# FNet mixing and a SoLU layer on one core: u transposed by block turns and block transfers instead of on TensorE

## The chip, the cores and the metric

The kernel runs on one core of a Trainium2 chip. The metric is the device time of one execution in microseconds (us); the median of three executions is 1578.13 (1572.94 to 1578.56). The engines are named as in the profile: PE is TensorE (PEld its weight loads), DVE is VectorE, ACT is ScalarE, POOL is GpSimd, and SP issues transfers. SP's transfers are also called its DMA queue (SPq).

## The reference

The input x has 8 sequences of 3136 rows with 256 features. The first block is the real part of a Fourier transform over rows and features. Its result, 25088 tokens of 256 features, goes through a layer of width 1024:

```
X = np.fft.fft(x, axis=1);  X = np.fft.fft(X, axis=2);  t = X.real
h = t @ w_in                                # 256 -> 1024
sm = softmax(h);  solu = h * sm
ln = (solu - mean) / sqrt(var + 1e-06) * g_ln
out = ln @ w_out                            # 1024 -> 256
```

## The kernel before, in words

All arithmetic is float32. The transform over 3136 = 49 x 64 rows is done in two steps. `transform1` (lines 134 to 157) works on a pair of sequences: 16 slices, each two matmuls against the table F; its result goes to DRAM (zd) and comes back turned (`turn`, lines 159 to 164: four transfers into g). `transform2` (166 to 176) is a matmul for each k1 of 25, and gives q, the stationary operand of the next matmul. The feature transform is folded into the weights Wi before the main loop. As x is real, the outputs for k1 and 49 - k1 come from the same q: an even and an odd part of h are computed, and their sum and difference are the two "signs" of a unit. So a unit is one pair of sequences and one k1, that is 128 tokens for each of two signs (for k1 = 0 one sign). There are 4 pairs x 25 units = 100 units.

For each unit: `up` (193 to 199) makes the two parts of h in PSUM (128 x 1024 each, one buffer each); `even` (201) copies the even part to SBUF; `join` (207) adds and subtracts on VectorE and takes the row maximum; `expo` (219) is the exponential on ScalarE, written to u; `product` (226) is u = h * u on VectorE, with its row sum; `square` (236) is ScalarE's sum of squares; `stats` (243) makes the row factor rs on GpSimd. The down product needs u with its 1024 features on the partitions. `transpose` (257 to 271) does that on TensorE: eight matmuls of 128 x 128 against an identity into PSUM, then two copies to SBUF (one ScalarE, one VectorE), giving uT. `down` (273) multiplies uT by Wo: eight matmuls with uT as the stationary operand and 256 moving columns; each float32 matmul stands as two in the profile. `store` (279) scales by rs and writes out: sign 0 by two plain transfers on SP's queue, sign 1 by an indirect transfer (scatter) on GpSimd's queue.

The order is written out by hand: instructions run on each engine in the order in which the loop of lines 421 to 460 issues them. A step of that loop does `up`, `join`, `expo`, `product` and `square` of the current unit, and `transpose`, `down` and `store` of the unit before it. Beside them it spreads the next pair's work (lines 383 to 402): `load` (94) brings a chunk of CH = 8 row positions twice, xa by a plain transfer and the mirrored xb by an indirect one; `add_mirror` (116) adds them on GpSimd; `fold` (124) folds the features on VectorE. Before the loop, the same is done for the first pair while the weights are prepared on VectorE (355 to 378).

## Time and profile before

| what | value |
|---|---|
| median of three runs | 1578.13 us (1572.94 to 1578.56) |
| time of the profiled execution | 1575.18 us |
| its span, first to last instruction | 1573.4 us |
| mean granted clock of TensorE | 0.969 |
| first and last start of `even` (L204) | 138.9 us, 1540.0 us |
| idle time of PE before L276 that ends with DVE's ot (L282) | 42.7 us |
| DMA packets, bytes | 45911, 84.72 MB |

A line of a group gives the line of the kernel, the engine, the operation, output <- inputs, the tile sizes and the count; behind the bar stand busy time in all, the mean of one in ns, and the idle time just before with what ended it. A line of the timeline gives start, duration, engine, line and operation, and in brackets the idle time before it with its releaser. Rows of the chain of waits give start, duration and what the chain went through. Rows of a window give its bounds and length, then busy time and count for PE, PEld, DVE, ACT and POOL, the granted clock, the mean busy share of the 16 DMA engines, and GB/s. Rows of a DMA queue give packets, MB and the share of the 16 engines' time. Matmuls overlap, so their rate is read from start to start.

### The profile page before, as it was taken

Reading aid. Unit: us, or ns where it says so; the run is one execution under the profiler, and the core shown is the slowest. Engines: PE = TensorE matmul, PEld = TensorE weight load, DVE = VectorE, ACT = ScalarE, POOL = GpSimd, SP = SyncE. Lnnn points to the kernel's source line nnn. Section 1 sums busy time; section 2 is a strip of 40 time slices with the busy share of each in tenths; the row PEclk is TensorE's granted clock in tenths of the full one; section 3 lists DMA queues with packets and bytes.
Section 4 is the critical chain, followed back from the end, with each engine's and each line's share of the span. In section 5 each row is a group of like instructions: output and inputs, shape, how many; then the busy total and the mean of one; then the engine's idle time right before and its main releaser. Section 6 shows DMA issues by size and latency. Waiting matters only on the chain.

```text
span 1573.4 us, 17844 instructions
## 1 busy us (share of the span) xinstructions
PE 1372.6 (87%) x6432; PEld 1043.2 (66%) x6432; DVE 965.8 (61%) x1725; ACT 621.2 (39%) x1049; POOL 413.0 (26%) x846
## 2 busy tenths in 40 slices
PE   2335999999999899999999899999999999999996
PEld 1213677777777677777777677777777677777775
DVE  3695656566655666565655756665655666666663
ACT  1101344344443443444443434434444434444442
POOL 3200323323213314223222324133212222221221
PEclk9667999999999999999999999999999999999998
DMA  9641212101052302101043402011023000000000
GB/s 230 201 85 41 59 38 64 39 21 38 18 111 75 96 20 82 38 21 38 21 89 65 129 18 85 22 34 38 21 70 72 18 21 21 20 17 21 19 19 20
DMA packets 45911, 84.72 MB, mean 54 GB/s; under 512 B 10390, under 2 KB 36638, under 8 KB 40832
## 3 DMA queue, kind: packets, MB, share of 16 engines
q1 hardware_dynamic: 33200, 52.64, 13.4%
q0 software_dynamic: 6656, 25.44, 5.2%
q10 hardware_dynamic: 5968, 5.52, 1.6%
q8 instruction: 50, 0.82, 0.2%
q14 instruction: 37, 0.30, 0.1%
HBM read 44.77 MB, written 38.80 MB: 53 GB/s over the span
## 4 chain that ended last, share of the span: by engine, by line
PE 56%; DVE 24%; issue 9%; ACT 8%; DMA 2%; DVEq 1%; POOL 1%; POOLq 0%; SPq 0%; ACTq 0%
PE ps_o L276 24%; PE ps_h L198 22%; DVE h L212 14%; ACT u L223 7%; PE tp L264 6%; PE ps L152 4%; DVE ot L282 2%; DVE ex L303 1%; DVE neg L217 1%; DMA xa<-in_x_dram 1%; DMA xb<-in_x_dram,idx 1%; DVE u L231 1%; POOL xa L121 1%; DVE rest L331 0%; DVE rest L333 0%
## 5 line engine op out<-in xcount | busy, mean ns | idle before, releaser
L276 PE MATMUL ps_o<-Wo,uT 128*128 128x256 f32 x3136 | 721.1, 383 | 44.7 <-DVE ot L282 42.7
L276 PEld LDWEIGHTS ps_o<-Wo,uT 128*128 128x128 f32 x3136 | 591.3, 191 | 181.5 <-issue 61.4
L223 ACT ACTIVATE u<-h,neg 128x1024 f32<-128x1024 f32 x196 | 223.6, 1142 | 434.3 <-DVE neg L217 434.3
L198 PE MATMUL ps_h<-Wi,q 128*128 128x512 f32 x800 | 379.2, 597 | 14.7 <-DVE q L180 14.7
L231 DVE SCALAR_TENSOR_TENSOR u<-h,u 128x1024 f32<-128x1024 f32 x196 | 239.2, 1220 | 130.9 <-ACT u L223 130.9
L233 POOL TENSOR_SCALAR nmean<-usum 128x1 f32<-128x1 f32 x196 | 55.8, 285 | 938.2 <-DVE u L231 938.1
L212 DVE CUSTOM_DVE_ANT_0 h<-ev,ps_h 128x1024 f32<-128x1024 f32 x196 | 231.7, 1219 | 81.6 <-PE ps_h L198 81.6
L240 ACT ACTIVATE h<-u,nmean 128x1024 f32<-128x1024 f32 x196 | 225.1, 1148 | 101.6 <-POOL nmean L233 99.0
L264 PEld LDWEIGHTS tp<-ident,u 128*128 128x128 f32 x1568 | 184.6, 142 | 62.3 <-issue 52.6
L270 ACT COPY uT<-tp 128x512 f32<-128x512 f32 x196 | 112.7, 575 | 280.8 <-PE tp L264 280.8
L282 DVE TENSOR_SCALAR ot<-ps_o,rs 128x256 f32<-128x256 f32 x196 | 94.4, 482 | 209.5 <-PE ps_o L276 209.5
L198 PEld LDWEIGHTS ps_h<-Wi,q 128*128 128x128 f32 x800 | 144.6, 191 | 117.5 <-issue 100.7
L264 PE MATMUL tp<-ident,u 128*128 128x128 f32 x1568 | 204.1, 273 | 0.0
L204 DVE SCALAR_TENSOR_TENSOR ev<-w_mid,q,ps_h 128x1024 f32<-128x1024 f32 x100 | 128.1, 1281 | 119.8 <-PE ps_h L198 119.8
L152 PE MATMUL ps<-y,F 98*100 98x258 f32 (+3 forms) x288 | 75.1, 398 | 81.5 <-DVE y L114 42.6
L268 DVE COPY uT<-tp 128x512 f32<-128x512 f32 x196 | 133.8, 683 | 1.2 <-PE tp L264 1.2
L285 POOL DMA_INDIRECT out_dram<-ot,idx x96 | 102.9, 1072 | 71.1 <-DVE ot L282 41.8
L152 PEld LDWEIGHTS ps<-y,F 98*100 98x100 f32 x288 | 44.0, 176 | 96.9 <-DVE ot L282 43.0
L121 POOL TENSOR_TENSOR xa<-xa,xb 98x2040 f32<-98x2040 f32 (+1 forms) x16 | 70.0, 4374 | 27.3 <-DMA xa<-in_x_dram 15.3
L255 POOL TENSOR_TENSOR rs<-v,neg_half 128x2 f32<-128x2 f32 (+1 forms) x100 | 71.8, 718 | 7.8
L172 PE MATMUL ps<-T,g 128*128 128x128 f32 x400 | 61.0, 275 | 0.0
L172 PEld LDWEIGHTS ps<-T,g 128*128 128x128 f32 x400 | 53.0, 191 | 0.7 <-issue 0.5
(57 smaller groups left out, 537.5 us busy)
## 6 DMA issues: line engine op xcount, KB each, us to landing
zd<-z SPq DMA_DIRECT2D x16, 800.0 KB
g<-zd SPq DMA_DIRECT2D x16, 800.0 KB
out_dram<-ot SPq DMA_DIRECT2D x200, 64.0 KB
xa<-in_x_dram SPq DMA_DIRECT2D x16, 784.0 KB
raw_in_moe_w_in_dram<-in_moe_w_in_dram ACTq DMA_DIRECT2D x1, 2048.0 KB
raw_in_moe_w_out_dram<-in_moe_w_out_dram ACTq DMA_DIRECT2D x1, 2048.0 KB
out_dram<-ot,idx POOLq DMA_INDIRECT x96, 2.5
T<-in_t_tab_dram ACTq DMA_DIRECT2D x2, 400.0 KB
```

Source lines behind the costliest of these rows:

```text
L152: nc.tensor.matmul(o[..., cs], F[:, 2 * t + h, :], i[..., cs], start=first, stop=True, skip_group_check=True)
L172: nc.tensor.matmul(ps[:, h * P : (h + 1) * P], pr.g[:, k1, h * P : (h + 1) * P], T[:, k1, :], start=(h == 0), stop=True, skip_group_check= ...
L198: nc.tensor.matmul(ps[:, fs], t.q[:, c * P : (c + 1) * P], Wi[:, c, fs], start=True, stop=True)
L204: nc.vector.scalar_tensor_tensor(out=t.ev, in0=w_mid, scalar=t.q[:, KD * P :], in1=ps, op0=ALU.mult, op1=ALU.add)
L212: nc.vector.tensor_tensor_reduce(out=t.h[s], in0=t.ev, in1=ps, scale=1.0, scalar=-3.0e38, op0=ALU.subtract if s else ALU.add, op1=ALU.max, ...
L223: nc.scalar.activation(out=t.u[s], in_=t.h[s], func=ACT.Exp, bias=t.neg[:, s : s + 1], accum_out=t.esum[:, s : s + 1])
L231: nc.vector.scalar_tensor_tensor(out=t.u[s], in0=t.h[s], scalar=1.0, in1=t.u[s], op0=ALU.mult, op1=ALU.mult, accum_out=t.usum[:, s : s + 1])
L240: nc.scalar.activation(out=t.h[s], in_=t.u[s], func=ACT.Square, bias=t.nmean[:, s : s + 1], accum_out=t.ssq[:, s : s + 1])
L264: nc.tensor.matmul(tp[:, c, :], t.u[s][:, f * P : (f + 1) * P], ident, is_transpose=True, start=(c == 0), stop=(c == n - 1), skip_group_ch ...
L268: nc.vector.tensor_copy(out=o, in_=tp)
L276: nc.tensor.matmul(ps, uT[:, c, :], Wo[:, c, :], start=(c == 0), stop=(c == KF - 1))
L282: nc.vector.tensor_scalar(out=ot, in0=ps, scalar1=t.rs[:, s : s + 1], scalar2=None, op0=ALU.mult)
```

## The change

- u is transposed in two parts. `turn_blocks`: one VectorE instruction per sign transposes every 32 x 32 block of u (128 x 1024) in place of its block row and writes it into a tile v of 128 x 1024 x 2, in which the two signs alternate; for k1 = 0 the one sign is written twice. `move_blocks`: 16 transfers from SBUF to SBUF on SP's queue put the blocks where they belong; each takes 32 partitions x 8 pieces of 64 floats (256 bytes) from block row i and column group q to partitions 32q of uT. So one set of 16 transfers serves both signs.
- `down` reads uT at every second element (sign s) as the stationary operand, and works on the unit of two steps before instead of one. The loop has one step more at its end. The identity matrix, the PSUM buffers for transposes and both copies of uT are gone; the pool ps_m has four buffers instead of two, u has two instead of four, uT three, v two.
- The copy of q out of PSUM and the scaling in `store` move from VectorE to ScalarE.
- CH is 4 instead of 8: eight chunks of half the size per pair. `ahead` and `ahead_pe` are set out anew: `add_mirror` on even steps from 2, `fold` on odd steps from 3, a slice of `transform1` in each of steps 4 to 19, `turn` in step 20 (it was step 21).

```
-CH = 8
+CH = 4
...
-    ps_t = ctx.enter_context(tc.tile_pool(name="ps_t", bufs=2, space=PSUM))
-    ps_m = ctx.enter_context(tc.tile_pool(name="ps_m", bufs=2, space=PSUM))
+    ps_m = ctx.enter_context(tc.tile_pool(name="ps_m", bufs=4, space=PSUM))
...
     def take2(ps):
         q = qpool.tile([P, KD * P + 1], FP32, tag="q", name="q")
-        nc.vector.tensor_copy(out=q, in_=ps)
+        nc.scalar.copy(q, ps)
         return q
...
-            t.u[s] = fpool.tile([P, FF], FP32, tag="u", name="u", bufs=4)
+            t.u[s] = fpool.tile([P, FF], FP32, tag="u", name="u", bufs=2)
...
-    def transpose(t, s):
...
-    def down(t, uT):
+    def turn_blocks(t, s):
+
+        if s == 0:
+            t.v = fpool.tile([P, FF, 2], FP32, tag="v", name="v32", bufs=2)
+        nc.vector.transpose(out=t.v[:, :, s], in_=t.u[s])
+        if len(t.signs) == 1:
+            nc.vector.transpose(out=t.v[:, :, 1], in_=t.u[s])
+
+    def move_blocks(t):
+
+        t.uT = fpool.tile([P, KF, 4, 64], FP32, tag="uT", name="uT", bufs=3)
+        v = t.v.rearrange("p (c q n) s -> p q c (n s)", q=4, n=32)
+        for i in range(4):
+            for q in range(4):
+                a, b = slice(32 * i, 32 * i + 32), slice(32 * q, 32 * q + 32)
+                nc.sync.dma_start(out=t.uT[b, :, i, :], in_=v[a, q])
+
+    def down(t, s):
+        uT = t.uT.rearrange("p c i (n s) -> p c (i n) s", s=2)
         ps = ps_m.tile([P, D], FP32, tag="m", name="ps_o")
         for c in range(KF):
-            nc.tensor.matmul(ps, uT[:, c, :], Wo[:, c, :], start=(c == 0), stop=(c == KF - 1))
+            nc.tensor.matmul(ps, uT[:, c, :, s], Wo[:, c, :], start=(c == 0), stop=(c == KF - 1))
         return ps
...
-        nc.vector.tensor_scalar(out=ot, in0=ps, scalar1=t.rs[:, s : s + 1], scalar2=None, op0=ALU.mult)
+        nc.scalar.mul(out=ot, in_=ps, mul=t.rs[:, s : s + 1])
...
-        c, r = divmod(step - 2, 5)
+        c, r = divmod(step - 2, 2)
         if step == 0:
             load(pr, 0)
             load(pr, 1)
-        if r == 4 and c + 1 < NC:
-            add_mirror(pr, c + 1)
-        elif 0 <= c < NC and r == 0:
-            fold(pr, c)
-            if c + 2 < NC:
-                load(pr, c + 2)
+        elif 0 <= c < NC:
+            if r == 0:
+                add_mirror(pr, c)
+            else:
+                fold(pr, c)
+                if c + 2 < NC:
+                    load(pr, c + 2)
...
-        if 0 <= c < NC and r:
-            transform1(pr, 4 * c + r - 1)
-            if c == NC - 1 and r == 4:
-                turn(pr)
+        if 0 <= step - 4 < NH // 2:
+            transform1(pr, step - 4)
+        elif step - 4 == NH // 2:
+            turn(pr)
...
             if cur:
                 even(cur, up(cur, 0))
                 odd = up(cur, 1)
+            if nxt:
+                nxt.q = take2(transform2(pairs[nxt.p], nxt.k1))
             if cur:
                 join(cur, odd)
                 expo(cur)
+            if ahd:
+                ahead_pe(ahd, cur.k1)
+            if old:
+                ps_o = [down(old, s) for s in old.signs]
             if cur:
+                for s in cur.signs:
+                    product(cur, s)
+                for s in cur.signs:
+                    square(cur, s)
+                    turn_blocks(cur, s)
+            if old:
+                store(old, 0, ps_o[0])
             if cur:
+                move_blocks(cur)
                 stats(cur)
+            if ahd:
+                ahead(ahd, cur.k1)
+            if old and 1 in old.signs:
+                store(old, 1, ps_o[1])
```

(old is the unit of two steps before, ahd the next pair; of the last piece, the new order of the loop is shown without the old one.)

Below are the rows of a step on the engines that the prediction speaks of, each with the line, the operation, output <- inputs and the shape; "x8" is eight alike in a row, and line numbers of the changed kernel are three lower. First TensorE in a step that carries a slice of the next pair's first transform (L152, L149), before:

```order
L198 MATMUL ps_h_6509<-Wi,q 128x512 x2
L264 MATMUL tp<-ident,u 128x128 x8
L198 MATMUL ps_h_6527<-Wi,q 128x512 x2
L276 MATMUL ps_o<-Wo,uT 128x256 x8
L264 MATMUL tp<-ident,u 128x128 x8
L172 MATMUL ps_6572<-T,g 128x128 x2
L174 MATMUL ps_6572<-g,T 128x1
L152 MATMUL ps_6580<-y,F 100x2x129
L152 MATMUL ps_6580<-y,F 100x2x127
L276 MATMUL ps_o<-Wo,uT 128x256 x8
```

and now:

```order
L195 MATMUL ps_h_6247<-Wi,q 128x512 x2
L195 MATMUL ps_h_6252<-Wi,q 128x512 x2
L169 MATMUL ps_6255<-T,g 128x128 x2
L171 MATMUL ps_6255<-g,T 128x1
L149 MATMUL ps_6274<-y,F 100x2x129
L149 MATMUL ps_6274<-y,F 100x2x127
L275 MATMUL ps_o<-Wo,uT 128x256 x16
```

The transposes (L264) are gone, and both down products stand together at the end of the step. Next VectorE in a step without folding, before:

```order
L204 SCALAR_TENSOR_TENSOR ev<-w_mid,q,ps_h_6004 128x1024
L268 COPY uT<-tp 128x512
L212 ISA h,nmax<-ev,ps_h_6022 128x1024
...
L217 TENSOR_SCALAR neg<-nmax 128x2
L231 SCALAR_TENSOR_TENSOR u,usum<-h,u 128x1024
L282 TENSOR_SCALAR ot<-ps_o,rs 128x256
L268 COPY uT<-tp 128x512
L180 COPY q<-ps_6067 128x257
L231 SCALAR_TENSOR_TENSOR u,usum<-h,u 128x1024
L282 TENSOR_SCALAR ot<-ps_o,rs 128x256
```

and now:

```order
L201 SCALAR_TENSOR_TENSOR ev<-w_mid,q,ps_h_5476 128x1024
L209 ISA h,nmax<-ev,ps_h_5481 128x1024
...
L214 TENSOR_SCALAR neg<-nmax 128x2
L228 SCALAR_TENSOR_TENSOR u,usum<-h,u 128x1024 x2
L258 STREAM_TRANSPOSE v_5519<-u 128x1024 x2
```

The five small operations on PSUM are gone from VectorE, and two block turns stand at its end. Last, SP's queue in step 20 of a pair, with the semaphores that each transfer waits for; DMAHW0 to DMAHW7 are counted up by the landing of SP's own transfers, in turn, DMASW by scatters:

```order
L160 DMA g<-zd 32x25x256 [waits DMAHW2_49]
L160 DMA g<-zd 32x25x256 [waits DMAHW3_49]
L160 DMA g<-zd 32x25x256 [waits DMAHW4_49]
L160 DMA g<-zd 32x25x256 [waits DMAHW5_49]
L289 DMA out_dram<-ot 64x256 [waits DMAHW6_49,DMASW0_49,Activation_49]
L289 DMA out_dram<-ot 64x256 [waits DMAHW7_49]
L269 DMA uT<-v_2522 32x8x64 [waits DMAHW0_49,DVE_49,PE_49]
L269 DMA uT<-v_2522 32x8x64 [waits DMAHW1_49]
L269 DMA uT<-v_2522 32x8x64 [waits DMAHW2_49]
L269 DMA uT<-v_2522 32x8x64 [waits DMAHW3_49]
```

Each transfer waits for the landing of the transfer eight before it, and the loads of g stand ahead of the step's store and of its 16 moves.

More of the change, by code (lines that the diff above doesn't have):

```diff
@@ L408 @@
         ahead(pairs[0], 0)
-        make_identity(nc, ident)
         nc.vector.memset(ones, 1.0)
@@ L422 @@
         units[0].q = take2(transform2(pairs[0], 0))
-        for i in range(len(units) + 1):
+        for i in range(len(units) + 2):
             cur = units[i] if i < len(units) else None
             nxt = units[i + 1] if i + 1 < len(units) else None
-            prv = units[i - 1] if i else None
-            two = prv is not None and 1 in prv.signs
+            old = units[i - 2] if i > 1 else None
+            ahd = pairs[cur.p + 1] if cur and cur.p + 1 < NP else None
             if cur:
                 even(cur, up(cur, 0))
-            if prv:
-                uT = transpose(prv, 0)
-            if cur:
                 odd = up(cur, 1)
-            if prv:
-                ps0 = down(prv, uT)
+            if nxt:
+                nxt.q = take2(transform2(pairs[nxt.p], nxt.k1))
             if cur:
```

36 lines of the change are left out of this document (removed).

## The prediction

> **What bounds the kernel now.** I read the page's busy shares first, then one period of the chain of waits in the last quarter of the run, where no loads run beside the units, and then the timeline of the same work.
>
> ```profile
> span 1573.4 us, 17844 instructions
> PE 1372.6 (87%) x6432; PEld 1043.2 (66%) x6432; DVE 965.8 (61%) x1725; ACT 621.2 (39%) x1049; POOL 413.0 (26%) x846
> PE 56%; DVE 24%; issue 9%; ACT 8%; DMA 2%; DVEq 1%; POOL 1%; POOLq 0%; SPq 0%; ACTq 0%
> ```
> ```profile
> 1258.66 3.69 PE ps_o L276 x16
> 1262.35 1.72 PE ps_h L198 x4
> 1264.07 0.87 PE tp L264 x8
> 1264.94 1.73 PE ps_h L198 x4
> ...
> 1272.46 3.69 PE ps_o L276 x16
> ```
> One unit takes 1272.46 - 1258.66 = 13.80 us. The chain follows TensorE for 8.0 us, then VectorE and ScalarE until the next down product may start. The timeline shows that TensorE works in most of that second part too:
>
> ```profile
> 1305.49 1.28 DVE L204 SCALAR_TENSOR_TENSOR ev<-w_mid,q,ps_h 128x1024 f32<-128x1024 f32 x1 [1.23 <-PE ps_h L198]
> 1307.88 3.62 PE L276 MATMUL ps_o<-Wo,uT 128*128 128x256 f32 x16
> 1308.18 1.22 DVE L212 CUSTOM_DVE_ANT_0 h<-ev,ps_h 128x1024 f32<-128x1024 f32 x1 [0.81 <-PE ps_h L198]
> 1310.59 0.17 DVE L217 TENSOR_SCALAR neg<-nmax 128x2 f32<-128x2 f32 x1
> 1311.34 1.04 PE L264 MATMUL tp<-ident,u 128*128 128x128 f32 x8
> 1312.06 1.23 DVE L231 SCALAR_TENSOR_TENSOR u<-h,u 128x1024 f32<-128x1024 f32 x1 [1.31 <-ACT u L223]
> 1312.21 0.61 PE L172 MATMUL ps<-T,g 128*128 128x128 f32 x4
> 1312.66 0.28 PE L174 MATMUL ps<-g,T 128*128 128x1 f32 x2
> 1313.84 3.69 PE L276 MATMUL ps_o<-Wo,uT 128*128 128x256 f32 x16 [0.90 <-DVE ot L282]
> ```
> From start to start TensorE spends 1311.34 - 1307.88 = 3.46 us on the first down product, 0.87 on a transpose, 0.45 + 0.28 on the transform of the next unit, waits 0.90, then 3.5 on the second down product. So TensorE is busy in 12.9 of 13.8 us: it is the bound, with one short wait per unit. The start times of L204 frame the whole unit phase:
>
> ```profile
> L204 DVE SCALAR_TENSOR_TENSOR ev<-w_mid,q,ps_h x100: 1279/1281/1283, 138.9 to 1540.0; 128x1024 f32<-128x1024 f32 x100
> 652.43 1.28 DVE L204 SCALAR_TENSOR_TENSOR ev<-w_mid,q,ps_h 128x1024 f32<-128x1024 f32 x1 [1.23 <-PE ps_h L198]
> 667.16 1.28 DVE L204 SCALAR_TENSOR_TENSOR ev<-w_mid,q,ps_h 128x1024 f32<-128x1024 f32 x1 [1.23 <-PE ps_h L198]
> ```
> So 99 steps take 1401.1 us, 14.15 each; a step that also carries one slice of the next pair's first transform takes 667.16 - 652.43 = 14.73, that is 0.93 more.
>
> **TensorE after the change.** It loses both transposes, and the 0.90 us wait goes too: the down products now read blocks that are two steps old. What is left of a step is 3.5 + 3.46 (down) + 2 x 1.73 (up) + 0.73 (transform) = 11.15 us, and about 0.95 more where a first-transform slice runs. One thing could spoil it: the stationary operand of the down product is now read at every second element (uT holds the two signs interleaved).
>
> ```profile
> L276 PEld LDWEIGHTS ps_o<-Wo,uT 128*128 128x128 f32 x3136 | 591.3, 191 | 181.5 <-issue 61.4 <-ACT uT L270 47.7
> L303 DVE TENSOR_SCALAR ex<-ex 128x512 int32<-128x512 int32 x12 | 5.1, 427 | 0.4
> L303 DVE TENSOR_SCALAR ex<-raw_in_moe_w_in_dram 128x512 int32<-128x512 int32 x12 | 5.1, 422 | 0.1
> ```
> A weight load takes 191 ns and hides behind a matmul of 3.46/16 = 216 ns. Bounds: 191 (free) and 382 (half speed). The raw_in row reads at the same stride of 8 bytes and takes 422 ns against 427 dense, on VectorE at least, so I take it as free.
>
> **VectorE.** It loses two copies of uT, the copy of q and both scalings of ps_o (to ScalarE, which at 39% has room) and gains two block turns. Its chain in a step, from the rows: L204 about 1.2; from the first L212 to L231 1312.06 - 1308.18 = 3.9, with the wait for the exponential in it; two products 2.5; and two turns. A turn reads and writes 128x1024 floats: the dense operations of that size take 1.22 to 1.28 us, so 1.2 is the lower bound; 2.4, half rate for the write at a stride of 8 bytes, the upper. I take 1.2: sum 7.6 + 2.4 = 10.0 us, below TensorE's 11.15. Folding is the same work in halves; it adds about 1.5 us in 8 of 25 steps, which also carry TensorE's 0.95. [...]
>
> **The block moves** are the new work: 16 transfers of 64 KB per unit on SP's queue, each 32 partitions x 8 pieces of 256 bytes: 4096 pieces, 256 for each of 16 DMA engines. I price issuing and moving apart.
>
> ```profile
> L290 SPq DMA_DIRECT2D out_dram<-ot x200: 466/583/1685, 157.7 to 1557.9; - x100
> L157 SPq DMA_DIRECT2D zd<-z x16: 274/287/294, 36.8 to 1167.1; - x16
> DMA to landing us min/median/max: 2.4/2.5/11.2
> ```
> Issuing one takes 0.29 to 0.58 us; with 0.5 the 16 moves take 8 us and the two stores 1.1, of a step of 11.15. The landing row is that of the scatter (L285), 2.5 us, which I use for a move too. Eight semaphores go round among SP's transfers, so at most eight are open: 8 x 0.5 = 4 us is longer than 2.5, and this limit costs nothing while the DMA engines keep up. For moving, the nearest row is the load of T, also in pieces of 256 bytes, which has the DMA engines nearly to itself in this window of 2 us:
>
> ```profile
> DMA packets 967, 0.28 MB, mean 140 GB/s; under 512 B 963, under 2 KB 963, under 8 KB 963
> q10 hardware_dynamic: 963, 0.25, 108.1%
> ```
> 16 x 2.0 us / 963 = 33 ns per piece: 256 x 33 = 8.5 us per unit. Bounds come from two stores of 64 KB out of SBUF in pieces of 1 KB (window of 2 us):
>
> ```profile
> DMA packets 161, 0.14 MB, mean 70 GB/s; under 512 B 32, under 2 KB 160, under 8 KB 160
> q1 hardware_dynamic: 160, 0.13, 26.5%
> ```
> 26.5% of 32 engine-us is 8.5 us for 128 pieces, so 64 ns each (the other 32 packets are the short ones of the first row, which I leave out): a quarter of it, 16 ns, if only bytes count, and 64 if only pieces count. That is 4.1 to 16.4 us a unit. I take 33. [...]
>
> What else the engines do:
>
> ```profile
> 200.00:600.00 400.00, 375.86 (x1781) 287.05 (x1781) 246.57 (x426) 170.54 (x290) 118.57 (x235) 1.00 0.20 54
> 1200.00:1500.00 300.00, 279.92 (x1343) 216.40 (x1342) 186.55 (x326) 127.45 (x216) 66.72 (x175) 1.00 0.07 20
> ```
> 0.07 of 13.8 us is 1.0 us per unit for the stores; 0.20 - 0.07 is 1.9 more while the next pair is loaded. So the engines need 8.5 + 1.0 + 1.9 = 11.4 us of a loading step (12.1 where TensorE has a slice), and 9.5 of the others.
>
> **Slack of a move.** Counted from the first up product of a step, VectorE ends its second turn at 1.73 + 1.73 + 0.1 + 3.9 + 2.5 + 2.4 = 12.4 us; the store of the older unit stands ahead on SP, until about 13. The moves are issued until 21 and land at about 23.5. The down product that needs them starts at 2 x 11.15 + 4.2 = 26.5. That leaves 3 us.
>
> **The turn of the next pair** uses that up. In step 20 of a pair SP issues the four loads of g ahead of that unit's store and moves.
>
> ```profile
> DMA packets 1835, 1.85 MB, mean 184 GB/s; under 512 B 31, under 2 KB 1834, under 8 KB 1834
> q1 hardware_dynamic: 1834, 1.85, 98.3%
> ```
> In this window of 10.1 us the loads of g ran alone: 98.3% of 161.6 engine-us over 1834 pieces is 87 ns each, so 3200 pieces fill the engines for 17.4 us. SP is free for them at about 10 us into the step, so they end at 28; the moves behind them land some 8 us later, at 36, against 26.5. So a stall of about 10 us, three times: it is the one place where this change turns a hidden load into a wait. POOL's scatter waits for the store behind g as well, and behind it the means of the next unit; that runs beside the same stall.
>
> **Start and end.** The first unit starts at 138.9 after weight work on VectorE; half-size chunks change what precedes it:
>
> ```profile
> L112 DVE TENSOR_TENSOR y<-xa 98x1016 f32<-98x1016 f32 x16 | 19.4, 1213 | 40.4 <-POOL xa L121 40.4
> 1562.43 0.96 POOL L285 DMA_INDIRECT out_dram<-ot,idx  x1 [8.26 <-DVE ot L282]
> ```
> Eight chunks with two buffers make more round trips, but each is shorter; the 40 us that folding waits could go either way. I put it at zero, with 5 us either side. At the end, from the last L204 (about 1.9 us into its step): its moves land at 23.5 to 25, two down products run until 32, the scatter starts at 33.5, and the rest takes 1573.4 - 1562.4 = 11 as before: 42.5 us after L204, against 33.4 now.
>
> **Sum.** Loading pair: 25 x 11.15 - 3.5 (the first unit has one sign) + 16 x 0.95 + 10 = 300.5; three are 901. Last pair, 24 steps: 264. The first two steps have no down product and follow VectorE's chain: -2. Then 138.9 + 901 + 264 - 2 + 42.5 = 1344 us of span. The profiled execution took 1575.2 for its 1573.4; the median is 3 above that. So 1344 + 2 + 3 = 1349, call it **1350 us**, 14% below now.
>
> **Rivals.**
> *The train of moves is the bound, and the kernel is slower.* Place: SP's queue and the 16 engines; price: 256 pieces per unit and engine. A step of a loading pair now takes 13.80 + 16/25 x 0.93 = 14.4 us, so it decides from (14.4 - 2.9)/256 = 45 ns per piece, or 0.8 us per move where issuing sets the pace. Midway between 33 and 64 ns, at 48.5, a step takes 12.4 + 2.9 = 15.3 and in the last pair 13.4: 139 + 75 x 15.3 + 24 x 13.4 + 43 = 1650 us; at 64 ns, 139 + 75 x 19.3 + 24 x 17.4 + 43 = 2050. For it: the move reads and writes SBUF and touches only 32 partitions on each side. Against: T's row is of the same piece. Between 33 and 45 ns the train binds mildly: 38 ns gives steps of 12.6 and 10.7 (TensorE's 11.15 then), so 1400 to 1500 with the stalls.
> *VectorE becomes the bound*: a turn of 2.4 us makes its chain 12.4 us and folding 0.5 more: 75 x 12.9 + 24 x 12.4 - 10 + 139 + 45 = 1440 us. For it: the strided write, which no row shows. Still faster.
> *Weight loads at a stride*: at 286 ns, midway, a down matmul is paced by its load, 70 ns x 3136 = 220 us: 1570, no change; at 382, 166 ns x 3136 = 520: 1870. Against it stands only the VectorE row.
> That the transposes leave TensorE is certain from the diff, so no rival is given for that.
>
> **How the numbers follow.** TensorE-bound, 1310 to 1400: 0.50. VectorE-bound, near 1440: 0.14. Train binds mildly, 1400 to 1560: 0.12. Train binds, over 1586: 0.16. Strided weight loads: 0.08, of which 0.03 lie within 0.5% and 0.04 above. A measurement here tells 0.5% from nothing. So faster 0.77, same 0.03, slower 0.20. The range is 1300 to 1590: it takes the first three and the lower half of the weight-load case and leaves out about 0.2.
>
> **What would show it.** Right: steps of 11.2 us in the last pair, with down products back to back and no transposes between; three stalls of about 10 us before a down product some two steps after the loads of g; turn instructions of 1.2 us; packets of 256 bytes at about 33 ns. Wrong: a down product that waits for the moves in every step (train), VectorE without idle time before L204 (turns), weight loads above 216 ns (stride). If moves take under 20 ns a piece, the stalls shrink and 1310 is in reach.

## The result, and the profile after

The changed kernel takes 1484.3 us (median; 1481.0 to 1487.0) against 1575.5 for the kernel before on the same chip: a ratio of 0.942, 95% interval 0.9389 to 0.945. It is faster, by 5.8% where 14% was forecast. The number lies inside the range of 1300 to 1590, but the step on which the forecast rested, that TensorE sets the pace, is wrong. These are the lines of the page of the changed kernel that answer to those shown of the kernel before:

```profile
span 1482.5 us, 17170 instructions
PE 1223.0 (82%) x4864; PEld 916.3 (62%) x4864; DVE 961.7 (65%) x1481; ACT 613.8 (41%) x1149; POOL 471.9 (32%) x892
...
q1 hardware_dynamic: 471952, 157.61, 48.0%
...
SPq 44%; PE 30%; DMA 13%; DVE 6%; issue 5%; POOL 1%; ACT 1%; POOLq 0%; ACTq 0%; DVEq 0%
...
L275 PE MATMUL ps_o<-Wo,uT 128*128 128x256 f32 x3136 | 730.7, 393 | 161.9 <-DMA uT<-v 87.2
L275 PEld LDWEIGHTS ps_o<-Wo,uT 128*128 128x128 f32 x3136 | 628.4, 203 | 247.4 <-issue 149.6
...
L258 DVE STREAM_TRANSPOSE v<-u 128x1024 f32<-128x1024 f32 x196 | 233.0, 1228 | 0.1
```

In the chain, TensorE has gone from 56% to 30% and SP's sequencer from nothing to 44%. SP computes nothing: these are the times in which it issues transfers. The first part of the page has no row for SP, so its busy shares show no engine above 82% and don't name the limit. The view of SP's line for the moves, and its timeline in the last pair, do:

```profile
L269 SPq DMA_DIRECT2D uT<-v x1600: 585/609/1978, 148.2 to 1468.2; - x178
...
  PE ps_o L275: 95.0, 42
```
```profile
1300.01 10.04 SPq L269 DMA_DIRECT2D uT<-v  x15
1310.16 1.18 SPq L289 DMA_DIRECT2D out_dram<-ot  x2
1311.44 11.76 SPq L269 DMA_DIRECT2D uT<-v  x16
1323.32 1.18 SPq L289 DMA_DIRECT2D out_dram<-ot  x2
```

A move takes 609 ns to issue (minimum, median, maximum stand in the row), and the next starts 654 ns after it: 16 are 10.5 us. With two stores of 1.18 us together and the gaps between, a step of SP is 11.9 to 12.1 us without a hole; 1310.16 to 1323.32 is one with a single slow issue in it, 13.2. Down products waited 95 us for moves, 42 times. The chain shows how such a step ends:

```profile
1321.94 0.61 SPq L269
...
1322.60 2.17 DMA uT<-v
...
1324.90 1.11 PE ps_o L275 x4
```

The last move is issued, lands 2.17 us later, and the down product starts. The start times of VectorE's first operation of a unit frame the phases again:

```profile
L201 DVE SCALAR_TENSOR_TENSOR ev<-w_mid,q,ps_h x100: 1236/1280/1282, 140.2 to 1442.7; 128x1024 f32<-128x1024 f32 x100
```

| stretch, us | before | forecast | after |
|---|---|---|---|
| to the first L204 (L201 after) | 138.9 | 138.9 | 140.2 |
| first pair | 356.6 | 298.5 | 329.9 |
| second, third pair | 358.7, 358.8 | 300.5 each | 340.0, 339.8 |
| last pair, 24 steps | 327.0 | 264 | 292.7 |
| from the last L204 (L201) to the end | 33.4 | 42.5 | 39.8 |
| span | 1573.4 | 1344 | 1482.5 |

Start and end came as forecast. The 138 us that are missing lie in the steps: 28.7 in the last pair, where nothing but the 18 transfers of a unit runs on SP, and 110 in the three loading pairs.

The step after the loads of g is the longest of a pair: 27.2 us in the second. Here is SP's timeline in it, and then the stretches of 5 us, whose last three columns are the granted TensorE clock, the DMA share and GB/s:

```profile
749.36 3.98 SPq L160 DMA_DIRECT2D g<-zd  x4
753.45 5.09 SPq L289 DMA_DIRECT2D out_dram<-ot  x2
758.65 15.99 SPq L269 DMA_DIRECT2D uT<-v  x16
```
```profile
748.00:753.00 5.00, 2.84 (x17) 2.56 (x16) 2.89 (x6) 2.07 (x4) 0.00 (x0) 1.00 0.69 168
753.00:758.00 5.00, 5.00 (x25) 4.54 (x24) 4.31 (x6) 0.68 (x2) 0.00 (x0) 1.00 1.11 205
758.00:763.00 5.00, 4.08 (x15) 2.08 (x13) 1.28 (x1) 0.00 (x0) 0.00 (x0) 1.00 1.11 214
763.00:768.00 5.00, 0.00 (x0) 0.00 (x0) 0.00 (x0) 0.00 (x0) 0.00 (x0) 0.83 1.11 212
768.00:773.00 5.00, 0.00 (x0) 0.00 (x0) 1.50 (x3) 2.78 (x6) 2.13 (x7) 0.50 0.52 116
```

The DMA engines are full (1.11) for some 15 us, and SP falls 13 us behind: the four loads of g take it 4.0 us, the two stores 5.1 instead of 1.2, and the 16 moves 16.0 instead of 10.5. In 5.0 of the last 5.5 us nothing is issued: the fifth and the sixth move wait for the landing of the third and the fourth load of g, the transfers eight before them. SP's waits for landings of g over the whole run (us, times, longest):

```profile
SPq L269 <- DMA g<-zd: 14.0, 6, 3.2
```

That is 4.7 us in the mean of the three turns. TensorE stands still for 14.4 us here, from 762.1 to 776.5. When it starts again its clock is at half (0.50), and the two down products take 8.85 us instead of 7.15.

### The profile page after: what moved, and what is told of

It reads as the page before. It is cut to its first block, busy times and chain, and to the rows that moved or that the text cites. A ratio compares the mean times of both kernels' runs of the same rounds, so it can differ in the third digit from the quotient of the medians.

```text
span 1482.5 us, 17170 instructions
## 1 busy us (share of the span) xinstructions
PE 1223.0 (82%) x4864; PEld 916.3 (62%) x4864; DVE 961.7 (65%) x1481; ACT 613.8 (41%) x1149; POOL 471.9 (32%) x892
## 4 chain that ended last, share of the span: by engine, by line
SPq 44%; PE 30%; DMA 13%; DVE 6%; issue 5%; POOL 1%; ACT 1%; POOLq 0%; ACTq 0%; DVEq 0%
SPq L269 39%; PE ps_o L275 19%; PE ps_h L195 9%; SPq L289 4%; DMA uT<-v 4%; DMA g<-zd 3%; DMA xa<-in_x_dram 2%; DMA out_dram<-ot 2%; DVE ex L302 2%; PE ps L169 1%; DMA xb<-in_x_dram,idx 1%; POOL xa L118 1%; PE ps L149 1%; DVE h L209 0%; DVE rest L330 0%
## 5 line engine op out<-in xcount | busy, mean ns | idle before, releaser
L275 PEld LDWEIGHTS ps_o<-Wo,uT 128*128 128x128 f32 x3136 | 628.4, 203 | 247.4 <-issue 149.6
L195 PE MATMUL ps_h<-Wi,q 128*128 128x512 f32 x800 | 360.2, 593 | 4.0 <-DVE ev L201 2.5
L284 POOL DMA_INDIRECT out_dram<-ot,idx x96 | 114.6, 1194 | 605.1 <-DMA out_dram<-ot 395.2
L201 DVE SCALAR_TENSOR_TENSOR ev<-w_mid,q,ps_h 128x1024 f32<-128x1024 f32 x100 | 127.8, 1278 | 217.6 <-PE ps_h L195 217.3
L258 DVE STREAM_TRANSPOSE v<-u 128x1024 f32<-128x1024 f32 x196 | 233.0, 1228 | 0.1
L177 ACT COPY q<-ps 128x257 f32<-128x257 f32 x100 | 37.4, 374 | 253.8 <-PE ps L171 253.7
L230 POOL TENSOR_SCALAR nmean<-usum 128x1 f32<-128x1 f32 x196 | 84.0, 440 | 161.2 <-DVE u L228 159.3
L149 PE MATMUL ps<-y,F 98*100 98x258 f32 (+3 forms) x288 | 80.3, 419 | 41.1 <-DVE y L111 41.0
L281 ACT ACTIVATE ot<-ps_o,rs 128x256 f32<-128x256 f32 x196 | 83.9, 459 | 69.8 <-PE ps_o L275 69.7
L149 PEld LDWEIGHTS ps<-y,F 98*100 98x100 f32 x288 | 48.0, 191 | 54.7 <-DVE y L111 21.3
L118 POOL TENSOR_TENSOR xa<-xa,xb 98x1020 f32<-98x1020 f32 (+1 forms) x32 | 72.7, 2272 | 27.7 <-DMA xa<-in_x_dram 19.0
L249 POOL TENSOR_SCALAR v<-ssq 128x2 f32<-128x2 f32 (+1 forms) x100 | 25.0, 250 | 169.6 <-ACT h L237 169.6
L152 ACT COPY z<-ps 100x512 f32<-100x512 f32 x64 | 36.2, 569 | 36.5 <-PE ps L149 27.2
```

The source lines that it names most:

```text
L149: nc.tensor.matmul(o[..., cs], F[:, 2 * t + h, :], i[..., cs], start=first, stop=True, skip_group_check=True)
L195: nc.tensor.matmul(ps[:, fs], t.q[:, c * P : (c + 1) * P], Wi[:, c, fs], start=True, stop=True)
L201: nc.vector.scalar_tensor_tensor(out=t.ev, in0=w_mid, scalar=t.q[:, KD * P :], in1=ps, op0=ALU.mult, op1=ALU.add)
L258: nc.vector.transpose(out=t.v[:, :, s], in_=t.u[s])
L275: nc.tensor.matmul(ps, uT[:, c, :, s], Wo[:, c, :], start=(c == 0), stop=(c == KF - 1))
L284: nc.gpsimd.indirect_dma_start(out=out, out_offset=bass.IndirectOffsetOnAxis(ap=idx[:, i : i + 1], axis=0), in_=ot, in_offset=None)
```

## The experiments

Two theories were left by the profile. **Issue**: the 0.65 us that SP needs for each transfer sets the step, whatever is in it. **Pieces**: the 4096 short pieces of a unit set it, and the issues are slow because of them. The first three runs tell these apart.

**One transfer a unit.** The whole of v goes to uT in one transfer of 128 rows of 8 KB, so that a block stays in its place within a row.

```
-        for i in range(4):
-            for q in range(4):
-                ...
-                nc.sync.dma_start(out=t.uT[b, :, i, :], in_=v[a, q])
+        nc.sync.dma_start(out=t.uT.rearrange("p c j n -> p (c j n)"), in_=t.v.rearrange("p m s -> p (m s)"))
```

> Leaves out the right placing of the blocks: one transfer of 128 x 8 KB copies v to uT, so the bytes moved per unit stay at 1 MB and the output is that of misplaced blocks. Theory (SP's issuing is the bound: 16 x 0.65 us for the moves plus 1.4 for the stores = 11.9 us a step): SP needs under 3 us a step, TensorE's 11.15 us becomes the step of the last pair (12.1 now), and the whole takes 1340 to 1390 us, depending on what the turn of the next pair still costs. Rival (the step is held by VectorE, ScalarE or the chain between engines): steps stay near 12 us and the time near 1480. Rival (DMA engines): steps shorten too, but packets of 8 KB fill the engines as long as before.

Measured: 1294.1 us, ratio 0.8213 (0.8177 to 0.8249).

```profile
L271 PE MATMUL ps_o<-Wo,uT x3136: 377/379/631, 153.9 to 1284.1; 128*128 128x256 f32 x196
L265 SPq DMA_DIRECT2D uT<-v x100: 482/536/552, 147.0 to 1272.5; - x100
```

Steps of the last pair take 11.0 us, 11.9 with a slice of the first transform, and the step of g 13.3. So everything else of the change does what the forecast said: TensorE's step (11.15 forecast), VectorE's turns, the strided weight load. What is missing in the changed kernel is in the moves.

**Sixteen transfers of big pieces.** As many transfers and bytes, but 32 pieces of 2 KB in each, where the changed kernel has 256 of 256 bytes; the blocks then end in other places of uT.

```
-        v = t.v.rearrange("p (c q n) s -> p q c (n s)", q=4, n=32)
+        v = t.v.rearrange("p (q m) s -> p q (m s)", q=4)
+        w = t.uT.rearrange("p (i c) j n -> p i (c j n)", i=4)
...
-                nc.sync.dma_start(out=t.uT[b, :, i, :], in_=v[a, q])
+                nc.sync.dma_start(out=w[b, i, :], in_=v[a, q])
```

> Leaves out the right placing of the blocks: still 16 transfers of 64 KB between the same partitions, but each of 32 pieces of 2 KB instead of 256 pieces of 256 bytes. Theory A (a transfer costs SP 0.65 us whatever its pieces): no change, 1484 +- 10, issues still 0.61 us. Theory B (SP waits while 256 pieces are described, 2.4 ns each): issues of 0.3 to 0.4 us, SP at 7 to 8 us a step, and 1350 to 1400 us. [...]

Measured: 1436.6 us, ratio 0.9117 (0.9078 to 0.9155).

```profile
L270 SPq DMA_DIRECT2D uT<-v x1600: 507/589/1693, 147.5 to 1420.0; - x178
```

**Eight transfers of small pieces.** As many bytes and pieces of 256 bytes, in half as many transfers (512 pieces in each); here too the blocks end in other places.

```
-        for i in range(4):
+        for i in range(2):
             for q in range(4):
-                a, b = slice(32 * i, 32 * i + 32), slice(32 * q, 32 * q + 32)
-                nc.sync.dma_start(out=t.uT[b, :, i, :], in_=v[a, q])
+                a, b = slice(32 * q, 32 * q + 32), slice(32 * (q ^ 1), 32 * (q ^ 1) + 32)
+                nc.sync.dma_start(out=w[b, i], in_=v[a, i])
```

> Leaves out the right placing of the blocks: 8 transfers of 128 KB with 512 pieces of 256 bytes, so pieces and bytes per unit are those of the changed kernel and the count of transfers is half. Theory A (cost per transfer): issues stay near 0.61 us, SP at 8 x 0.65 + 1.4 = 6.6 us a step, TensorE-bound steps of 11.15 and 1350 to 1400 us. Theory B (cost per piece): issues of about 1.2 us, SP still near 11.5 us a step, 1460 to 1484.

Measured: 1325.5 us, ratio 0.8412 (0.8376 to 0.8448).

```profile
L270 SPq DMA_DIRECT2D uT<-v x800: 585/642/3941, 146.9 to 1305.9; - x160
```

An issue takes 589 ns with 32 pieces, 609 with 256 and 642 with 512: it is a price of a transfer, to which a piece adds about 0.1 ns. Eight times fewer pieces are worth 48 us (1484.3 - 1436.6), half as many transfers 159 (1484.3 - 1325.5). **Issue** holds, and with eight transfers the forecast's sum (1344 of span) is met by a span of 1323.

If SP's issuing is the limit, part of the moves can go to another queue. Two runs put four of the sixteen on ScalarE.

**The last four moves on ScalarE** (i = 3), and, after that brought nothing, **the first four** (i = 0):

```
-                nc.sync.dma_start(out=t.uT[b, :, i, :], in_=v[a, q])
+                eng = nc.scalar if i == 3 else nc.sync
+                eng.dma_start(out=t.uT[b, :, i, :], in_=v[a, q])
```

> 4 of the 16 moves (those out of the last block row) are issued from ScalarE's queue, the rest from SP's. Theory (SP's issuing is the bound): SP at 12 x 0.65 + 1.4 = 9.2 us a step, ScalarE at 41% has room for 2.6 more, so steps of the last pair at 11.2 to 11.4 and 1380 to 1410 us. Rival (one generator behind both queues, or landing): issues grow to 0.8 us or more and the time stays within 10 of 1484.

> The changed kernel with the first four of a unit's 16 moves (i = 0) issued by ScalarE, ahead in program order of the twelve that SP issues; the run with the last four on ScalarE brought nothing (ratio 1.0005 to the kernel before), because the eight landing semaphores go round over both queues in program order and SP's moves waited for moves that ScalarE issued late. Theory (SP's issue rate is the limit, and that run failed only by the order): SP then has 12 x 0.65 + 1.4 = 9.2 us a step, under TensorE's 11.15; steps of 11.2 to 11.5 us and a shorter turn step, 1350 to 1390 us. Rival (the shared round of eight couples the two queues whatever the order, since ScalarE issues its four only when its own work lets it): steps of 12 us or more, alternating, 1450 to 1580. In both the moves keep 0.6 us each to issue.

Measured: 1578.3 us, ratio 1.0005 (0.9982 to 1.0028), for the one, and 1578.3, ratio 1.0015 (0.9993 to 1.0037), for the other: both take back the whole gain. The issues themselves take no longer on two queues (610 and 622 ns in the median, against 609 on SP alone); of the first run:

```profile
L270 SPq DMA_DIRECT2D uT<-v x1200: 585/610/2037, 149.0 to 1566.9; - x172
L270 ACTq DMA_DIRECT2D uT<-v x400: 592/622/1767, 149.0 to 1556.0; - x134
```

But SP now waits for landings, which it hardly did in the changed kernel outside the turn of g (its moves waited 2.0 us for each other in the whole run). The second run, in the last pair: SP's waits from 1230 to 1540 us, then ScalarE's and SP's timeline.

```profile
SPq L270 <- DMA uT<-v: 87.0, 23, 6.2
```
```profile
1411.57 14.11 SPq L270 DMA_DIRECT2D uT<-v  x12
1421.49 0.59 ACTq L270 DMA_DIRECT2D uT<-v  x1
1423.63 2.05 SPq L270 DMA_DIRECT2D uT<-v  x3
```

SP issued nine moves of a unit by 1417.5 and then stood until 1423.63, which is 2.14 us, one landing, after ScalarE's first move at 1421.49; and so in every second step, where a step of 11.0 alternates with one of 16. The order of the program says why: the eight landing semaphores are handed out over both queues in the order in which the scheduler merges them, and it puts the moves that ScalarE makes for the *next* unit between SP's for this one. SP's rows of a unit, and ScalarE's moves of the next:

```
L270 DMA uT_9055<-v32_9047 32x8x64 [waits DMAHW6_49]
L270 DMA uT_9055<-v32_9047 32x8x64 [waits DMAHW0_49]
L270 DMA uT_9055<-v32_9047 32x8x64 [waits DMAHW2_49]
L270 DMA uT_9055<-v32_9047 32x8x64 [waits DMAHW4_49]
L270 DMA uT_9055<-v32_9047 32x8x64 [waits DMAHW6_49]
L270 DMA uT_9055<-v32_9047 32x8x64 [waits DMAHW7_49]

L270 DMA uT_9144<-v32_9136 32x8x64 [waits DMAHW4_49,DMAHW2_49,DMAHW7_49,DMAHW0_49,DVE_49]
L270 DMA uT_9144<-v32_9136 32x8x64 [waits DMAHW1_49]
L270 DMA uT_9144<-v32_9136 32x8x64 [waits DMAHW3_49]
L270 DMA uT_9144<-v32_9136 32x8x64 [waits DMAHW5_49]
```

Semaphores 7, 1, 3 and 5, left out between SP's 6, 0, 2, 4 and 6, are those of the next unit's moves. SP's tenth move waits for 7, that is for a move that ScalarE can only issue when the next unit is turned and squared. So the first expectation fell, and the second with it: putting these moves first in the program doesn't put them first in the round.

**Four moves on POOL.** POOL's scatters count another semaphore up (DMASW0, in the row of a store in step 20), so moves on POOL should stay out of that round.

```
-                nc.sync.dma_start(out=t.uT[b, :, i, :], in_=v[a, q])
+                eng = nc.gpsimd if i == 3 else nc.sync
+                eng.dma_start(out=t.uT[b, :, i, :], in_=v[a, q])
```

> The changed kernel with the last four of a unit's 16 moves (i = 3) issued by POOL, whose landing semaphores are a set of their own, so that its queue is not coupled to SP's as ScalarE's was in the two runs that brought nothing. Theory (SP's issue rate is the limit): SP has 12 x 0.65 + 1.4 = 9.2 us a step, POOL 4 x 0.78 = 3.1 more (0.78 is what a load of g took to issue there), TensorE sets the pace with 11.1: the last pair takes 24 x 11.1 = 266 us instead of 293, a loading pair 25 x 11.1 + 16 x 0.95 + 16 for the turn = 309; 140 + 3 x 309 - 10 + 266 + 38 = 1360, 1340 to 1390. Rival (POOL issues moves more slowly, or its other work waits behind them, the means of the next unit first): steps stay at 12 or more, 1450 to 1520.

Measured: 1348.3 us, ratio 0.8548 (0.8523 to 0.8574). The moves on both queues, and TensorE's timeline in the last pair:

```profile
L270 SPq DMA_DIRECT2D uT<-v x1200: 585/610/2083, 148.2 to 1330.4; - x172
L270 POOL DMA_DIRECT2D uT<-v x400: 582/596/717, 148.8 to 1322.8; - x134
```
```profile
1201.81 7.16 PE L276 MATMUL ps_o<-Wo,uT 128*128 128x256 f32 x32
1208.80 3.60 PE L195 MATMUL ps_h<-Wi,q 128*128 128x512 f32 x8
...
1212.82 7.16 PE L276 MATMUL ps_o<-Wo,uT 128*128 128x256 f32 x32
```

From 1201.81 to 1212.82 is a step of 11.01 us with TensorE back to back, the picture that the prediction drew. 136 us come from moving a quarter of the issues: with 12 moves a step of SP is 9.2 us, under TensorE's 11. Here the step of g is 24.8 us, a stall of 13.8.

**What makes the stall of g.** The loads of g on POOL's queue instead of SP's:

```
-            nc.sync.dma_start(out=pr.g[j * NH : (j + 1) * NH, :, :],
+            nc.gpsimd.dma_start(out=pr.g[j * NH : (j + 1) * NH, :, :],
```

> The changed kernel with the four loads of g issued by POOL instead of SP; everything else as it is. Theory (SP's queue sets the pace, and the loads of g are a stall in it): a loading pair of the changed kernel takes 340 us, 25 steps of about 12 are 300 and the step of the turn is 27 of them, so without g ahead of the moves the three turn steps fall from 27 to about 13 us: 3 x 14 = 42 us less, about 1440; ordinary steps stay at 12.1, since the 16 moves and two stores are still 11.9 us of SP. Rival (POOL is as bad a place: it issues the scatters whose landing was waited for, and g's 3200 pieces keep the 16 DMA engines busy for 17 us wherever they are issued): the moves behind are late all the same, 1470 to 1485, no change against the changed kernel.

Measured: 1485.8 us, ratio 0.9429 (0.9397 to 0.9461), the changed kernel's time; the theory missed. The long step is there (30.1 us in the second pair), though SP issues nothing of g. POOL issues the four loads from 743.26 to 746.36, while SP issues the 16 moves for which the next down product waits:

```profile
738.05 17.05 SPq L269 DMA_DIRECT2D uT<-v  x16
```

They take 17.05 us instead of 10.5, 6.9 of them for the last two, and that down product starts 9.7 us after the last issue instead of 2.3. Two stretches behind it:

```profile
753.00:758.00 5.00, 0.00 (x0) 0.00 (x0) 1.37 (x4) 0.03 (x1) 0.00 (x0) 0.50 1.08 220
758.00:763.00 5.00, 0.00 (x0) 0.00 (x0) 0.00 (x0) 0.00 (x0) 0.00 (x0) 0.50 1.12 188
```

The engines are as full (1.08 and 1.12) as when SP loaded g. So the stall doesn't need the place in SP's queue: the 3200 pieces of g and the moves share the DMA engines wherever they are issued. POOL is a bad place of its own, too: its scatter waits 15.4 us there for the landing of a store, so the run doesn't show what the full engines cost alone. The next step was to spread the loads in time:

```
-        elif step - 4 == NH // 2:
-            turn(pr)
+        elif 0 <= step - 4 - NH // 2 < 4:
+            turn(pr, step - 4 - NH // 2)
```

(turn then issues only the load j that it is given.)

> The changed kernel with the four loads of g issued one in each of the steps 20 to 23 of a pair instead of all four in step 20; still on SP. The run with g on POOL's queue kept the long step (27 to 30 us), and its DMA engines were full (share 1.07 to 1.12) for some 17 us of it. Theory (the 3200 pieces of g, in front of the moves in the engines, are the stall): 800 pieces at a time are 4.4 us of the engines in a step in which they have room, so the long step of 27 us becomes four of 12 to 14: 3 x 10 to 14 = 30 to 42 us less, 1440 to 1455. Rival (the long step has another cause, such as the wait for zd at its start): 1475 to 1485.

> Both of these in one kernel: four moves of a unit on POOL, and the loads of g one in each of four steps. Theory: 1360 less 3 x 12 for the turn steps, 1325; 1300 to 1350, faster than the kernel before and the changed kernel. Rival: the two gains lean on the same time and add to less, 1360 to 1450.

Measured: 1462.1 us, ratio 0.9272 (0.9244 to 0.9299), for the spread loads alone. That lies between the two expectations, nearer to the theory. The step of 27 us is gone, but the second and the third pair take 331 us, 8.5 less and not 10 to 14, and the first takes 329.9 as it did. SP has no room in the steps into which the loads went (15.6 and 15.5 us in the second pair), and the last step of a pair is now 18.6: the six steps from step 20 on are only 2 to 4 us shorter, and the rest of the gain lies in steps that load nothing of g and was not explained. With four moves on POOL as well it is 1331.7 us, ratio 0.8442 (0.8412 to 0.8472), as the sum of the two said, and the best kernel here that computes the same: 15.6% under the kernel before. Here, where SP has room, the spreading takes 6 us off those six steps in every pair. The last step of a pair is the long one now, 18.7 to 19.5 us, because TensorE waits there for the last load of g:

```profile
PE ps L169 <- DMA g<-zd: 17.2, 3, 6.5
```

**The two steps.** The changed kernel with its down products one step later:

```
-        for i in range(len(units) + 2):
+        for i in range(len(units) + 1):
...
-            old = units[i - 2] if i > 1 else None
+            old = units[i - 1] if i > 0 else None
```

> The changed kernel with its down products one step later, as in the kernel before, instead of two (units[i - 1] in the loop; one step fewer at the end). Theory: from the first up product of a unit its turns end at about 12.4 us, 16 moves at 0.65 us follow and land at 12.4 + 10.5 + 2.5 = 25.4, the two down products take 7 us, and only then may the up products of the unit after next start: 32.4 us for two steps, 16.2 a step, 139 + 75 x 16.4 + 24 x 16.2 + 3 x 15 + 40 = about 1840 us; 1750 to 1850, slower than the kernel before, with TensorE waiting for uT in every step. Rival (the delay is worth little, since SP's issue rate sets the pace anyway): steps stay near 12, 1480 to 1520.

Measured: 2214.8 us, ratio 1.4049 (1.3999 to 1.4099): slower by far more than the 1750 to 1850 expected. The chain in the last pair is one ring, from one landing (first line) to the first move of the next unit (last line):

```profile
1725.47 2.13 DMA uT<-v
...
1727.94 6.38 PE ps_o L275 x16
1734.34 0.48 ACT ot L281
1734.85 0.52 SPq L289
1735.41 0.60 SPq L289
...
1736.11 0.64 SPq L269
```

Sixteen moves, a landing, a down product, its scaling, its store, and only behind the store on SP the next unit's moves: 10.5 + 2.1 + 6.4 + 0.5 + 1.1 is 20.6, and steps take 20.4. I had left the store out of the ring, and the down product takes 6.38 us here, not 3.5: the granted clock is 0.60 to 0.70 in these stretches (0.815 over the span). With 16 moves on SP and the down products only one step later, the turn on VectorE loses 40% against the kernel before; the second step is a part of the change that nothing else in it makes up for.

**The chunks alone.** The kernel before with CH = 4 and the steps of the changed kernel's ahead and ahead_pe (as in the diff above).

> The kernel before with the half-size load chunks alone (CH = 4, with the changed kernel's steps for loading, folding and first transform); transposes on TensorE, down products one step later. Both the forecast (zero, with 5 us either side) and its rival ask whether the chunks carry any of the 91 us that the change gained. Theory: none, 1565 to 1587. Rival: they carry 2% or more either way, under 1545 or over 1607.

Measured: 1565.7 us, ratio 0.9926 (0.9904 to 0.9948). That is 0.7% or 12 us less: more than the 5 us that the forecast allowed either side, less than the rival. But it isn't all of the chunks' making. Of the 8.9 us between the profiled executions, 7.0 lie behind the last L204, where no chunk is loaded: at the end of the program SP waits for the sequencer of PE, in the kernel before

```profile
SPq L532 <- PEq L532: 7.8, 2, 7.3
```

and in this run, as in the changed kernel, only 0.8. What that wait hangs on was not examined. About 7 us of the 91 that the change gained are of the same kind, and for the chunks themselves a few us are left.

**Through DRAM.** Five transfers a unit instead of sixteen: v is written to DRAM in one, and read back in four one step later. For whole pieces of 2 KB the elements are laid out so that turn and weight load go in strides of 64 bytes.

```
+        v = t.v.rearrange("p q n c s -> p c q n s")
...
+        nc.sync.dma_start(out=t.vd, in_=t.v.rearrange("p q n c s -> p q (n c s)"))
...
+        for q in range(4):
+            nc.sync.dma_start(out=w[32 * q : 32 * q + 32], in_=vd[q])
```

> The same turns, with the blocks carried in 5 transfers a unit instead of 16: one write of v to DRAM, and one step later, ahead of that step's store, four reads of it into uT (32 partitions each, pieces of 2 KB). For that v and uT hold a block's elements interleaved over the eight column groups, so that the turn writes and the weight load reads at a stride of 64 bytes instead of 8. Down products two steps later as in the changed kernel, g still on SP. Theory (issue per transfer is the limit): SP has 5 x 0.65 + 1.4 = 4.7 us a step, TensorE sets the pace with 11.0 to 11.2, the turn step stalls by 5 to 10 us: 1310 to 1350. Rivals: the round trip is late (write issued at 13 us, landed at 19, reads landed at 26 against a down product at 26.5, so any delay is a wait in every step): 1400 to 1500; the stride of 64 bytes slows the turn to 2.4 us (1440) or the weight load beyond 216 ns (1570 and more); the turn's and weight load's rows tell these apart.

Measured: 1455.6 us, ratio 0.9235 (0.921 to 0.9261). Faster than the changed kernel, but not the 1310 to 1350 expected. The time is that of the first rival (the round trip is late); the stride slowed both rows, and cost little.

```profile
L281 PEld LDWEIGHTS ps_o<-Wo,uT 128*128 128x128 f32 x3136 | 721.2, 307 | 132.5 <-issue 113.5 <-PE ps L171 1.9 <-ACT ot L287 1.6
L260 DVE STREAM_TRANSPOSE v<-u 128x1024 f32<-128x1024 f32 x196 | 363.0, 1925 | 0.1
```
```profile
1271.13 7.44 PE ps_o L281 x32
```
```profile
PE ps_o L281 <- DMA uT<-vd: 28.6, 12, 9.8
SPq L154 <- ACT z L152: 70.3, 8, 10.2
```

The turn takes 1.93 us and the weight load 307 ns, where a stride of 8 bytes gave 1.23 and 203. Yet the last pair's steps are 11.4 us, close to TensorE's 11.0: 32 matmuls of the down products take 7.44 us instead of 7.16, though 32 loads of 307 ns add up to 9.8, so the loads as recorded overlap and don't set the pace. The loss is in the loading pairs, 13.4 a step: from 480 to 790 us down products wait 28.6 us for blocks that come back late (in the last pair a write and a read land 5.7 us each after their issue). One reason stands in SP's order: its write of zd waits for ScalarE's copy of z, 70 us in the same stretch (last row), and the four reads stand behind it. How much of the rest of those steps is the stride's and how much the round trip's was not separated.

## Why the prediction was right or wrong

**What bounds it after the change: wrong.** The forecast was TensorE with 11.15 us a step, and the sum itself stands: 11.0 us wherever the moves are out of the way (one transfer a unit, eight transfers, four moves on POOL). The step that failed is that SP issues a unit's 16 moves and two stores in 9.1 us, inside TensorE's step; it needs 11.9, and so SP sets the pace. It fell because of one term:

- *"with 0.5 the 16 moves take 8 us and the two stores 1.1, of a step of 11.15"*. The rows quoted there ran from 0.29 to 0.58 us; I took a value inside them for a transfer of a kind that none of them showed. Measured 0.609, and 0.654 from start to start: 10.5 us and 1.4 with the gaps for the stores, 11.9. TensorE would have stayed the bound up to (11.15 - 1.4)/16 = 0.61 a move, so 0.5 against 0.65 decided the whole forecast. Even the upper of the rows quoted would have shown it: 18 issues of 0.583, with the 0.05 us that stand between two stores in the trace of the kernel before, are 11.4 us, already more than 11.15.
- The text bounded a piece from both sides and the time of an issue from neither; the slow rival had its issue condition ("0.8 us per move"), but between 0.61 and 0.8 lay a mild case of its own that I gave only to pieces ("38 ns gives ... 1400 to 1500"). That the measured time is in that rival's range is luck: its cause is another.

**The moving: right side, wrong size, without effect.** 33 ns a piece was taken, 18 is measured: in a window of 6 us of the changed kernel with moves and a scatter, 46.0% of 96 engine-us over 2432 packets.

```profile
q1 hardware_dynamic: 2432, 0.59, 46.0%
```

That is near the lower bound of 16 (its 8.5 us over 128 pieces are 66 ns and not 64, so 17), and the engines are half idle (0.49 from 1200 to 1450 us). So bytes count here; the price of short pieces, taken from T's load out of DRAM, is not seen between SBUF and SBUF. With fewer issues the text's own "under 20 ns ... 1310 is in reach" comes near: eight transfers of the same pieces gave 1325.5, one transfer 1294.1.

**VectorE and the stride: right.** The turn takes 1.228 us (1.2 taken of 1.2 to 2.4), the weight load 203 ns in the mean and 196 in the median, hidden behind its matmul. Neither rival had anything. But the price of the second was too high: it let a weight load longer than 216 ns set the pace, and with loads of 307 ns through DRAM two down products took 0.28 us longer, not 2.9.

**The stall of g: right in kind, small in size.** About 10 us were forecast, three times; it was 15 in the changed kernel and 13.8 with four moves on POOL. With eight transfers it was 9, with one transfer about 2, so the same four loads cost the more, the more moves SP has to issue beside them. The text put it down to the place in SP's queue and to the engines' 17.4 us alike. The run with g on POOL shows that the full engines delay the moves without that place; in the changed kernel the delay comes about on SP, by slow issues and by waits for the landing of g.

**Loading pairs: a part was missing.** Beside the slower moves and g's stall, SP issues eight loads of xa and eight writes of zd in each pair; the text listed queues and DMA share for the loads, but no issue time for them. The median issues are 0.526 and 0.472 us, 8 us a pair, and between the first L201 of the second and of the third pair SP's 471 issues add up to 307 us and the time between them to 33, of 340 (21 of the 33 are the gaps of 0.045 us behind each, 5 the waits for g). With an SP that has no free time every such issue lengthens the pair.

**Semaphores: right in ordinary steps, missed in the turn.** "This limit costs nothing while the DMA engines keep up" holds for SP's moves alone (they wait 2.0 us for each other in the whole run). In the turn the engines don't keep up, and the limit costs SP 14.0 us; with ScalarE's queue in the same round it ate the whole gain.

**Start and end: right** within 3 us, the end by luck. The last scatter starts 35.8 us after the last L201 and not 31.6, and what follows it takes 4.0 us and not the 11 taken over from the kernel before, in which 7.3 were the wait for PE's sequencer. The chunks, put at zero with 5 us either side, gave 12 us on the kernel before, 7 of them by that same wait.

## What to carry to other kernels

Count transfers as instructions of the queue that issues them: so many by the time from one issue to the next (0.65 us here), in every step, and compare that with the busiest engine before comparing bytes; a page whose chain of waits has its largest share in a queue's sequencer (44% here), while no engine is above 82%, says just this. Work that is cut into many small transfers wants fewer transfers (eight instead of sixteen were worth 159 us) or a second queue (four moves on POOL, 136 us), and in these runs the second queue helped on POOL (ratio 0.855), whose scatters were counted apart from SP's transfers, and not on ScalarE (1.000), whose moves shared SP's round: read in the program's order which earlier landing each transfer waits for. Here the large load beside the short moves filled the DMA engines (1.07 to 1.12) and delayed the moves from either queue (16 took 16.0 and 17.05 us to issue instead of 10.5), and on their own queue they also waited for its landing (14.0 us in three turns). Spread over steps it cost less, the more where the queue had room in them: 6 us off the six steps from step 20 on in every pair, and 2 to 4 where it had none.

## What was not expected of the hardware

- The time to issue a transfer within SBUF hardly depended on its pieces: 589 ns in the median with 32, 609 with 256, 642 with 512. It was much the same on SP (610), ScalarE (622) and POOL (596), also with two of them issuing in one run.
- Pieces of 256 bytes from SBUF to SBUF took 18 ns of an engine, half of what pieces of that length took in the load of T from DRAM (33). Pieces of 2 KB in as many transfers took about 130, an estimate: 43.7% of 16 engines over a span of 1433.9 us, less the 13.4% of 1573.4 that SP's queue took in the kernel before, over 51200 pieces. So the short ones cost hardly more for their bytes.
- A stride of 8 bytes cost VectorE's turn nothing that shows (1.23 us, where dense operations of that size took 1.22 to 1.28) and TensorE's weight load little (196 ns in the median against 190); at 64 bytes the turn went from 1.23 to 1.93 us and the weight load from 203 to 307 ns, which still cost the matmuls only 4% (7.44 us against 7.16).
- The stalls cost more than their length: after 14.4 idle us TensorE went on at a granted clock of 0.50, and two down products took 8.85 us instead of 7.15. In the kernel that stalled in every step (granted clock 0.60 to 0.70) sixteen matmuls took 6.38 us instead of 3.5.
